# Sinkhorn attention and max-out layer on one core: W2 turned by DMA instead of TensorE, its loads gated, and the first item in another order

## The chip, the core and the metric

The kernel runs on one NeuronCore of a Trainium2 chip. The metric is the time on the device in microseconds, the median of several executions. A NeuronCore has five engines with instruction streams of their own, joined by semaphores: TensorE (PE; PEld is its weight load), VectorE (DVE), ScalarE (ACT), GpSimd (POOL) and SyncE (SP). Sixteen DMA engines move data between HBM, the main memory, and SBUF, the memory on the core; GpSimd and SyncE issue almost all of the DMAs here. Matmuls write to PSUM, from where DVE or ACT copies results to SBUF.

## The reference

```python
P = sort_net                                   # (4, 8, 8, 8)
for _ in range(5):
    P = exp(P - max(P, -1))
    P = P / (sum(P, -1) + 1e-9)
    P = P / (sum(P, -2) + 1e-9)
k_sorted = einsum('bhij,bhjcd->bhicd', P, k_b) # k, v: (4, 8, 768, 64) in 8 blocks of 96
v_sorted = einsum('bhij,bhjcd->bhicd', P, v_b)
attn = softmax(q_b @ k_sorted^T / 8)           # within each block of 96
x = (attn @ v_sorted) -> (3072, 512)           # heads side by side
out = maximum(x @ w1, x @ w2) @ w_out          # w1, w2: 512 x 1024, w_out: 1024 x 512
```

All inputs and the output are float32; the kernel's matmul operands are bfloat16, cast during the loads.

## The kernel before, in words

The batch has four items (b = 0 to 3); each gives 768 tokens. The work of one item is this chain:

- `sort_k(b, t)`, t = 0 to 2: 32 small matmuls that multiply k by a block-diagonal matrix made from P (L458), and a copy to kT (DVE or ACT). The t-th sort needs only the t-th third of the loaded k.
- `turn_v` reorders v within each partition (L245 on ACT, L250 on DVE), and `sort_v`, `sort_v_pair` or `sort_v_halved` sort it (L479, L523, L500). A sort of v takes single columns out of all 96 rows of a block, so it needs every turn.
- `q_transposes`: on TensorE for items 0 and 1 (L433), by DMA for items 2 and 3 (L419).
- `scores(b, u)`, u = 0 to 7 (L548), the exponential on ACT (L556), `values(b, u)` (L575), and the division on DVE (L586, L592), which gives x. The first four u belong to the first half of the tokens, the last four to the second.
- `x_transposes(b, t)`: on TensorE for item 0 (L613), by DMA on SP's queue for the others (L605). Two u make one t. The products of the first token half need t = 0 and 1, those of the second t = 2 and 3.
- `moe_h(b, ch, t)` (L677), then `moe_out(b, ti, part)` (L704).

The layer uses max(h1, h2) = relu(x(W1 - W2)) + x W2. So W2 is subtracted from W1 in SBUF (`w_difference`, L231, by quarters of 256 columns: two on GpSimd, two on DVE), relu is taken of the products, and W2 W_out is made once as the matrix wc (`w_product(dmt)`, L657) and applied to x next to W_out. For `w_product`, W2 must be transposed (w2T). In the kernel before, `w2_transposes(t, eng)` does that: 16 matmuls of 128 columns against the identity (L638) and one copy of 2048 columns by `evac`, for each half of W2's 1024 columns (steps tw0 and tw1).

Everything stands in program order by hand; each engine takes its instructions in that order. `evac` gives a copy to ACT or DVE by a running load count unless an engine is named. PSUM has four tiles for everything (`ps`).

The stages, with what sets their order:

- The start: five sinkhorn rounds on DVE and ACT (`sinkhorn(it)`, L264 to L283), with ACT turning v of item 0 between them. TensorE multiplies zeros meanwhile (`keep_streaming`, L82): 86 matmuls of 126 columns, then six of 512 columns in each of the last two rounds. GpSimd issues, in this order, v, k and q of item 0, then after two mask copies (L763) the first two quarters of W2 and W1, the selections, the other halves of both, W_out, two differences, and k of item 1 (L767 to L777).
- The front: item 0, by the list `front` (L783 to L789): k, v sorts, tq q transposes, SC scores, VA values, tx x transposes, tw W2 transposes, h products with a letter a or b for the two halves of their accumulation, diff the differences on DVE, pe the block-diagonal matrices of the other items, and F zeros of 512 columns put ahead of the next step that takes them. A trailing A or D names the engine of the copy. Before the last 26 steps, q of item 1, v of items 1 and 2 and k of item 2 are issued (L830 to L834); behind the front, q of item 2 into W2's buffer (L838).
- The rest: for each item, a list of units (L909 to L933). For item 0 there are eight empty ones, four of `w_product` (n = 8 to 11) and twelve of `moe_out` (n = 12 to 23); for the later items eight of `moe_h` and twelve of `moe_out`. Behind unit n the steps of a tail are put: `first_tail` holds item 1's attention and the sorting of v of items 1 and 2 (`sort_v_pair`), `second_tail` item 2's attention and v of item 3. KS is the three key sorts, TQ the q transposes, TURN the turns, VS the sorts of v, SC, VA and TR scores, values and x transposes.

All loads are issued by GpSimd, and so go through one queue of DMAs; outputs and transposing DMAs go through SP's.

Of the kernel before, what the change touches and what calls it, by code (L numbers as in the profile page):

```python
# [11 lines left out]
BF16 = mybir.dt.bfloat16  # L12
# [4 lines left out]
def kernel(  # L17
# [16 lines left out]
    nc = tc.nc  # L34
# [34 lines left out]
    def ps_bf16(name):  # L69
        return psum.tile([128, 2048], BF16, tag="ps", name=name)  # L70
# [48 lines left out]
    kT = {}  # L119
# [511 lines left out]
    w2T = big.tile([128, NFB, DMODEL], BF16, tag="w2T", name="w2T")  # L631
    wc = big.tile([128, HP, DMODEL], BF16, tag="wc", name="wc")

    def w2_transposes(t, eng):
        ps = ps_bf16("tw_ps")
        for n in range(16):
            fb, dmt = t * 4 + n // 4, n % 4
            nc.tensor.matmul(  # L638
                ps[:, n * 128 : (n + 1) * 128],
                w2_sb[:, dmt, fb * 128 : (fb + 1) * 128],  # L640
                ident,
                is_transpose=True,
                start=True,
                stop=True,
            )
        return lambda: evac(
            w2T[:, t * 4 : t * 4 + 4, :].rearrange("p f d -> p (f d)"),
            ps,
            2048,
            two_x=True,  # L650
            eng=eng,
        )

    def w_product(dmt):
# [95 lines left out]
        return SC, VA, TR  # L750

    first, second, both = slice(0, 64), slice(64, 128), slice(0, 128)
    keep_streaming(ps_f32("fill_ps"), 86 * 126, most=126)
    for it in range(5):
        sinkhorn(it)
        if it < 3:
# [5 lines left out]
    for c, n, m in [(2, 2, 0), (4, 3, 1)]:  # L762
# [1 line left out]
            out=maskJ[:, c : c + n],  # L764
            in_=maskJ[:, m].to_broadcast([128, NB, n]).transpose([0, 2, 1]),
        )
    for t in range(2):  # L767
        load_w_columns(w2_sb, moe_w2, t, t + 1)
        load_w_columns(w1_sb, moe_w1, t, t + 1)
    for b in range(1, B):  # L770
        selections(b)
    load_w_columns(w2_sb, moe_w2, 2, 4)
    load_w_columns(w1_sb, moe_w1, 2, 4)
    load_w(wo_sb, moe_w_out)
    w_difference(0, nc.gpsimd)
    w_difference(1, nc.gpsimd)
    load_k(1)  # L777
    turn_v(first, "A", 36, 56)
    turn_v(first, "A", 56, 80)
    block_diagonals_first()  # L780
    turn_v(first, "D", 80, 96)

    front = """  # L783
        k0D k1A k2D v1D v2A v3A tq0D v0A tq1D SC1 SC0 F1
        SC2 VA1 SC5 VA0 SC3 F2 VA2 SC4 F0 tx0D SC6 VA3
        SC7 h00a VA4 tx1A tw0D h01a VA5 h01bA diff2 h00bA VA7 tx2A
        tw1A h02a VA6 h02bA h11a diff3 tx3A h12a h03a h12bD h10a h10bA
        pe2 h11bD h03bA h13a h13bA
    """.split()  # L789
    fills = [0]  # L790

    def fills_due():
# [3 lines left out]
    def front_step(step):  # L796

        eng = step[-1] if step[-1] in "AD" else None
        name = step[:-1] if eng else step
        kind = name.rstrip("0123456789ab")  # L800
        n = [int(x) for x in name if x.isdigit()]
        if kind == "F":
            fills[0] = 512
        elif kind == "k":
            sort_k(0, n[0], 640 if step == front[0] else 0, eng)
        elif kind == "v":
            sort_v(0, n[0], 0, eng)
        elif kind == "tq":
            q_transposes(0, n[0], eng)
        elif kind == "SC":  # L810
            scores(0, n[0], fills_due())
        elif kind == "VA":
            values(0, n[0], fills_due())
        elif kind == "tx":
            x_transposes(0, n[0], eng)
        elif kind == "tw":
            w2_transposes(n[0], eng)()
        elif kind == "diff":
            w_difference(n[0])
        elif kind == "pe":  # L820
            block_diagonals([(0, 2), (0, 3), (1, 1), (1, 2), (1, 3)], 2)
        elif name[-1] == "a":
            moe_h_products(0, n[0], n[1], (0, 2), fills_due())
        else:
            moe_h(0, n[0], n[1], eng, (1, 3))

    for step in front[:-26]:
        front_step(step)

    load_q(1)  # L830
    for piece in range(2):
        for b in (1, 2):
            load_v(b, which=piece)
    load_k(2)  # L834

    for step in front[-26:]:
        front_step(step)
# [7 lines left out]
    def sorts_and_scores(b):  # L845
# [6 lines left out]
    TURN = [lambda c=c: turn(both, c) for c in (0, 24, 48, 72)]  # L852
    first_tail = {
        7: KS,
        9: [TQ[0], TURN[0]],
        10: [SC[0], TQ[1], TURN[1]],
        11: SC[1:4] + TURN[2:4] + [lambda half=half: load_v(3, half=half) for half in range(2)],
        12: VS[0:3],
        13: VS[3:6],
        14: VS[6:8] + [SC[4]],  # L860
        15: [VA[0], lambda: pair_q(2, 0)],
        16: [VA[1], lambda: pair_q(2, 1)],
        17: SC[5:8] + [TR[0]],
        18: [VA[2]],
        19: [VA[3], TR[1]],
        20: [VA[4]],
        21: [VA[5], TR[2]],
        22: [VA[6], VA[7], TR[3]],
    }
    SC, VA, TR, KS = sorts_and_scores(2)  # L870
    VS = [lambda t=t: sort_v_halved(3, t) for t in range(4)]
    TURN = [lambda c=c: turn(both, c) for c in (0, 24, 48, 72)]
    second_tail = {
        0: [lambda: q_transposes(2, 0), lambda: q_transposes(2, 1)],
        2: KS,
        4: SC[0:2],
        5: [VA[0]],
        6: SC[2:4] + [TURN[0]],
        7: [VA[1], TR[0]],
        8: [VA[2], TURN[1]],  # L880
        9: [VA[3], TR[1], TURN[2]],
        10: SC[4:7],
        11: [VA[4], TURN[3]],
        12: [VA[5], TR[2], lambda: load_k(3), lambda: load_q(3)],
        13: [VA[6]],
        14: SC[7:8] + VS[0:2],
        15: [VA[7], TR[3]],
        16: VS[2:4],
        17: [lambda: pair_q(3, 0)],
        18: [lambda: pair_q(3, 1)],  # L890
    }
    SC, VA, TR, KS = sorts_and_scores(3)
# [69 lines left out]
```

The softmax here doesn't subtract the row's maximum and nothing guards it: scores larger than these inputs give would overflow.

## Time and profile before

| | |
|---|---|
| median of 8 runs | 166.58 us (166.16 to 169.9) |
| the profiled execution's own time | 166.71 us |
| its span | 164.9 us |
| granted TensorE clock | 0.997 |
| instructions | 4563 |
| data moved by DMA | 23.90 MB, 145 GB/s over the span |
| loads, through GpSimd's queue | 11040 packets, 13.37 MB, 48.3% of 16 engines |
| outputs and transposing DMAs, through SP's queue | 19200 packets, 10.17 MB, 26.3% |

The span goes from the first to the last instruction of one profiled execution; the execution's own time is 1.8 us more. Times inside are microseconds from the span's start. The page cuts the span in 40 slices of 4.1 us; a digit is the busy share of a slice in tenths. The chain of work that ended last is followed back from the last instruction, at each step to what released it. "From issue to landing" is the time from the start of a DMA's issuing instruction until its data are there.

### The profile page before, as it was taken

What the parts mean: (1) busy time and instruction counts of PE and PEld (TensorE: products, weight loads), DVE (VectorE), ACT (ScalarE), POOL (GpSimd) and SP (SyncE); (2) the same over time, 40 slices, a digit from 0 to 9 for tenths busy, and PEclk for the clock granted to TensorE, in tenths of its full rate; (3) what the DMA queues carried; (4) which work ended last, traced back from release to release, by engine and by line L of the source; (5) the groups of instructions that cost most, each with busy time, mean ns of one, the idle gap of its engine ahead of it and who ended that gap; (6) DMA issues with size and microseconds to landing.
All of it is one profiled execution on the core that took longest, in us unless ns stands there. A gap on an engine that the chain in (4) does not pass through costs nothing.

```text
span 164.9 us, 4563 instructions
## 1 busy us (share of the span) xinstructions
PE 159.4 (97%) x2018; PEld 96.5 (59%) x2018; DVE 76.2 (46%) x169; ACT 83.1 (50%) x102; POOL 32.7 (20%) x59
## 2 busy tenths in 40 slices
PE   7999799999999999999999999999999999999992
PEld 7958578756555555557655554575655546654451
DVE  4869778546375574535277763250642420000011
ACT  3585894927239847055752353457447206642020
POOL 7989587140205000000014010000000000000000
PEclk9999999999999999999999999999999999999998
DMA  3999999999999995688425999990025294000333
GB/s 41 202 207 197 198 208 204 210 204 220 211 205 209 218 234 105 175 116 205 102 19 105 187 182 225 195 228 16 0 52 175 50 164 142 0 0 0 127 131 127
DMA packets 30405, 23.90 MB, mean 145 GB/s; under 512 B 16753, under 2 KB 25201, under 8 KB 30385
## 3 DMA queue, kind: packets, MB, share of 16 engines
q0 software_dynamic: 11040, 13.37, 48.3%
q1 hardware_dynamic: 19200, 10.17, 26.3%
q8 instruction: 16, 0.26, 0.6%
q10 hardware_dynamic: 144, 0.07, 0.1%
q14 instruction: 5, 0.03, 0.1%
HBM read 26.75 MB, written 6.29 MB: 200 GB/s over the span
## 4 chain that ended last, share of the span: by engine, by line
PE 95%; ACT 1%; issue 1%; DVE 1%
PE out_ps L704 38%; PE h_ps L677 26%; PE fill_ps L82 6%; PE o_ps L575 5%; PE wc_ps L657 4%; PE k_ps L458 4%; PE s_ps L548 4%; PE tq_ps L433 2%; PE v_ps L479 1%; PE v_ps L523 1%; PE tw_ps L638 1%; ACT e L556 1%; PE tx_ps L613 1%; PE v_ps L500 1%; DVE qT L110 1%
## 5 line engine op out<-in xcount | busy, mean ns | idle before, releaser
L704 PE MATMUL out_ps<-wo_sb,g 128*128 128x512 bf16 (+2 forms) x200 | 48.3, 371 | 0.1
L677 PE MATMUL h_ps<-xT,w_sb 128*128 128x384 bf16 x256 | 44.5, 326 | 0.0
L677 PEld LDWEIGHTS <-w_sb 128*128 128x128 bf16 x256 | 24.0, 98 | 15.6
L556 ACT ACTIVATE e<-s_ps 96x768 bf16<-96x768 f32 x32 | 23.9, 804 | 14.0 <-PE s_ps L548 13.8
L691 ACT ACTIVATE g<-h_ps 128x768 bf16<-128x768 f32 x27 | 21.8, 811 | 17.4 <-PE h_ps L677 17.3
L704 PEld LDWEIGHTS <-g 128*128 128x128 bf16 x200 | 17.1, 97 | 15.8
L704 PE MATMUL out_ps<-wc,xT 128*128 128x512 bf16 (+2 forms) x100 | 24.8, 370 | 0.0
L108 ACT COPY o<-out_ps 128x1024 f32<-128x1024 f32 x10 | 10.1, 1012 | 28.0 <-PE out_ps L704 25.2
L592 DVE TENSOR_TENSOR x<-o_ps,rs 96x512 bf16<-96x512 f32 x32 | 22.0, 687 | 1.1
L704 PEld LDWEIGHTS <-xT 128*128 128x128 bf16 x100 | 9.6, 97 | 11.2
L575 PEld LDWEIGHTS <-e 96*128 96x128 bf16 x256 | 11.8, 97 | 5.9 <-DVE v_sb L110 0.2
L586 DVE RECIPROCAL rs<-o_ps 96x8 f32<-96x8 f32 x32 | 6.4, 200 | 18.1 <-PE o_ps L575 17.9
L739 DVE COPY o<-out_ps 128x512 f32<-128x512 f32 (+1 forms) x2 | 1.2, 625 | 27.6 <-PE out_ps L704 27.6
L575 PE MATMUL o_ps<-v_sb,e 96*128 96x65 bf16 x256 | 12.9, 193 | 0.0
L110 DVE CAST kT<-k_ps 128x1024 bf16<-128x1024 f32 x7 | 8.3, 1216 | 9.3 <-PE k_ps L458 9.3
L108 ACT CAST v_sb<-v_ps 96x1024 bf16<-96x1024 f32 x10 | 9.8, 1013 | 2.4 <-PE v_ps L479 0.9
L693 DVE TENSOR_SCALAR g<-h_ps 128x768 bf16<-128x768 f32 x5 | 4.8, 956 | 10.8 <-PE h_ps L677 10.8
L110 DVE CAST v_sb<-v_ps 96x1024 bf16<-96x1024 f32 x6 | 7.3, 1218 | 5.1 <-PE v_ps L523 2.2
L548 PE MATMUL s_ps<-qT,kT 64*128 64x96 bf16 x256 | 8.6, 204 | 1.1 <-PE o_ps L575 0.8
L548 PEld LDWEIGHTS <-kT 64*128 64x128 bf16 x256 | 6.1, 94 | 5.9 <-issue 3.6
L160 POOL DMA_DIRECT2D v_raw<-in_k_dram x3 | 2.5, 833 | 35.2 <-DVE v_dc L250 31.4
L82 PE MATMUL fill_ps<-fill 128*128 128x126 bf16 x86 | 7.7, 278 | 1.2 <-DVE fill L73 1.2
(95 smaller groups left out, 143.3 us busy)
## 6 DMA issues: line engine op xcount, KB each, us to landing
out_dram<-o SPq DMA_DIRECT2D x11, 512.0 KB, 3.1
v_raw<-in_v_dram POOLq DMA_DIRECT2D x8, 384.0 KB, 12.5
k_raw<-in_k_dram POOLq DMA_DIRECT2D x9, 256.0 KB, 10.0
w_sb<-in_moe_w_dram POOLq DMA_DIRECT2D x4, 256.0 KB, 9.5
w_sb<-in_moe_w_dram POOLq DMA_DIRECT2D x2, 512.0 KB, 11.0
wo_sb<-in_moe_w_out_dram POOLq DMA_DIRECT2D x2, 512.0 KB, 14.5
v_raw<-in_v_dram POOLq DMA_DIRECT2D x3, 256.0 KB, 4.9
q_raw<-in_q_dram POOLq DMA_DIRECT2D x4, 192.0 KB, 9.1
```

Of the source, the lines that this page charges most:

```text
L82: nc.tensor.matmul(ps[:, 0:w], w0, fill[:, 0:w], start=True, stop=True)
L108: nc.scalar.copy(out=out_ap, in_=in_ap)
L110: nc.vector.tensor_copy(out=out_ap, in_=in_ap)
L458: nc.tensor.matmul(ps[r0 : r0 + 64, m * 64 : (m + 1) * 64], kv[r0 : r0 + 64, t * 16 + m, :], bd_k[b][r0 : r0 + 64, :], start=True, stop=True,)
L548: nc.tensor.matmul(ps[:, h2 * 512 + ii * 128 : h2 * 512 + ii * 128 + BLK], kT[b][rows, (hp * 8 + i) * BLK : (hp * 8 + i) * BLK + 128], rhs ...
L556: nc.scalar.activation(out=e[:, 0 : 8 * BLK].rearrange("p (t c r) -> p t c r", t=8, r=R), in_=ps[0:BLK] .rearrange("p (t f) -> p t f", t=8 ...
L575: nc.tensor.matmul(ps[:, h2 * 512 + ii * 65 : h2 * 512 + (ii + 1) * 65], e[:, (h2 * 4 + ii) * BLK : (h2 * 4 + ii) * BLK + 128], v_sb[:, m0 ...
L592: nc.vector.tensor_tensor(out=x, in0=ov[:, :, :, 0:D], in1=rs.to_broadcast([BLK, 2, 4, D]), op=ALU.mult,)
L657: nc.tensor.matmul(ps[:, 0:512], w2T[:, fb, dmt * 128 : (dmt + 1) * 128], wo_sb[:, fb, :], start=(fb == 0), stop=(fb == NFB - 1),)
L677: nc.tensor.matmul(h_ps[ch, t][:, m * 512 : m * 512 + TCH], w1_sb[:, hp, fb * 128 : (fb + 1) * 128], xT[:, b % 2, ch, hp % 2, hp // 2, :], ...
L691: nc.scalar.activation(out=g, in_=src, func=AF.Relu)
L704: nc.tensor.matmul(dst, g_tiles[b, ch, m // 2][:, m % 2, off : off + 128] if m < NFB else xT[:, b % 2, ch, hp % 2, hp // 2, off : off + 12 ...
```

## The change

- `w2_transposes(dmt)` becomes one DMA transpose on SP's queue: 128 rows (of the 512) of W2 by 1024 columns, for each of the four dmt, written to w2T. The steps tw0 and tw1, their 32 matmuls and their two copies go.
- GpSimd's loads are gated by three small copies to a new tile `seen`. The first reads the last sinkhorn result; behind it come the first quarter of W2 and the selections of items 1 and 2. The second reads the first sorted keys; behind it come the other loads of W1 and W2 (now the second half of W1 ahead of that of W2), the selection of item 3, W_out, the four transposes (on SP), the differences and k of item 1. The third reads the w2T columns that the second transpose writes; behind it come q of item 1 (now in four DMAs), v of items 1 and 2 (now in four pieces each) and q of item 2.
- k of item 2 is loaded later, behind unit 16 of item 0's units.
- The front list has another order, beginning with the second token half, and four F instead of three; F now adds up.
- The zeros at the start: 92 matmuls of 118 columns.
- The tails of items 0 and 1 are placed anew: of item 1's attention nearly everything stands later in the list of units.

```diff
--- before.py
+++ after.py
@@ -631,24 +631,10 @@
     w2T = big.tile([128, NFB, DMODEL], BF16, tag="w2T", name="w2T")
     wc = big.tile([128, HP, DMODEL], BF16, tag="wc", name="wc")
 
-    def w2_transposes(t, eng):
-        ps = ps_bf16("tw_ps")
-        for n in range(16):
-            fb, dmt = t * 4 + n // 4, n % 4
-            nc.tensor.matmul(
-                ps[:, n * 128 : (n + 1) * 128],
-                w2_sb[:, dmt, fb * 128 : (fb + 1) * 128],
-                ident,
-                is_transpose=True,
-                start=True,
-                stop=True,
-            )
-        return lambda: evac(
-            w2T[:, t * 4 : t * 4 + 4, :].rearrange("p f d -> p (f d)"),
-            ps,
-            2048,
-            two_x=True,
-            eng=eng,
+    def w2_transposes(dmt):
+        nc.sync.dma_start_transpose(
+            out=w2T[:, :, dmt * 128 : (dmt + 1) * 128],
+            in_=w2_sb[:, dmt, :],
         )
 
     def w_product(dmt):
@@ -750,7 +736,7 @@
         return SC, VA, TR
 
     first, second, both = slice(0, 64), slice(64, 128), slice(0, 128)
-    keep_streaming(ps_f32("fill_ps"), 86 * 126, most=126)
+    keep_streaming(ps_f32("fill_ps"), 92 * 118, most=118)
     for it in range(5):
         sinkhorn(it)
         if it < 3:
@@ -764,29 +750,24 @@
             out=maskJ[:, c : c + n],
             in_=maskJ[:, m].to_broadcast([128, NB, n]).transpose([0, 2, 1]),
         )
-    for t in range(2):
-        load_w_columns(w2_sb, moe_w2, t, t + 1)
-        load_w_columns(w1_sb, moe_w1, t, t + 1)
-    for b in range(1, B):
-        selections(b)
-    load_w_columns(w2_sb, moe_w2, 2, 4)
-    load_w_columns(w1_sb, moe_w1, 2, 4)
-    load_w(wo_sb, moe_w_out)
-    w_difference(0, nc.gpsimd)
-    w_difference(1, nc.gpsimd)
-    load_k(1)
     turn_v(first, "A", 36, 56)
     turn_v(first, "A", 56, 80)
     block_diagonals_first()
+    seen = const.tile([128, 3, 2], BF16, tag="seen", name="seen")
+    nc.gpsimd.tensor_copy(out=seen[0:G, 0], in_=p_bf[:, NB - 1, NB - 2 :])
+    load_w_columns(w2_sb, moe_w2, 0, 1)
+    selections(1)
+    selections(2)
     turn_v(first, "D", 80, 96)
 
     front = """
-        k0D k1A k2D v1D v2A v3A tq0D v0A tq1D SC1 SC0 F1
-        SC2 VA1 SC5 VA0 SC3 F2 VA2 SC4 F0 tx0D SC6 VA3
-        SC7 h00a VA4 tx1A tw0D h01a VA5 h01bA diff2 h00bA VA7 tx2A
-        tw1A h02a VA6 h02bA h11a diff3 tx3A h12a h03a h12bD h10a h10bA
-        pe2 h11bD h03bA h13a h13bA
+        k1A k0A v1D k2A v2A v0D tq0D v3A tq1D SC4 SC5 F2
+        F3 VA4 SC6 SC7 VA5 F0 SC0 VA6 SC1 VA7 F1 SC3
+        tx2D SC2 tx3D VA1 h10a VA0 VA2 h10bA h11a tx0A h11bA diff3
+        VA3 diff2 h13a h01a tx1D h03a h13bD h03bD h01bA h12a pe2 h00a
+        h02a h00bD h02bA h12bA
     """.split()
+
     fills = [0]
 
     def fills_due():
@@ -800,7 +781,7 @@
         kind = name.rstrip("0123456789ab")
         n = [int(x) for x in name if x.isdigit()]
         if kind == "F":
-            fills[0] = 512
+            fills[0] += 512
         elif kind == "k":
             sort_k(0, n[0], 640 if step == front[0] else 0, eng)
         elif kind == "v":
@@ -813,8 +794,6 @@
             values(0, n[0], fills_due())
         elif kind == "tx":
             x_transposes(0, n[0], eng)
-        elif kind == "tw":
-            w2_transposes(n[0], eng)()
         elif kind == "diff":
             w_difference(n[0])
         elif kind == "pe":
@@ -824,14 +803,29 @@
         else:
             moe_h(0, n[0], n[1], eng, (1, 3))
 
-    for step in front[:-26]:
+    front_step(front[0])
+    c0 = int(front[0][1]) * 16
+    nc.gpsimd.tensor_copy(out=seen[:, 1], in_=kT[0][:, c0 : c0 + 2])
+    load_w_columns(w1_sb, moe_w1, 0, 1)
+    load_w_columns(w2_sb, moe_w2, 1, 2)
+    selections(3)
+    load_w_columns(w1_sb, moe_w1, 1, 2)
+    load_w_columns(w1_sb, moe_w1, 2, 4)
+    load_w_columns(w2_sb, moe_w2, 2, 4)
+    load_w(wo_sb, moe_w_out)
+    for dmt in range(HP):
+        w2_transposes(dmt)
+    w_difference(0, nc.gpsimd)
+    w_difference(1, nc.gpsimd)
+    load_k(1)
+    nc.gpsimd.tensor_copy(out=seen[:, 2], in_=w2T[:, NFB - 1, 254:256])
+    for step in front[1:-26]:
         front_step(step)
 
-    load_q(1)
-    for piece in range(2):
+    load_q(1, True)
+    for piece in range(4):
         for b in (1, 2):
-            load_v(b, which=piece)
-    load_k(2)
+            load_v(b, 4, which=piece)
 
     for step in front[-26:]:
         front_step(step)
@@ -852,41 +846,39 @@
     TURN = [lambda c=c: turn(both, c) for c in (0, 24, 48, 72)]
     first_tail = {
         7: KS,
-        9: [TQ[0], TURN[0]],
-        10: [SC[0], TQ[1], TURN[1]],
-        11: SC[1:4] + TURN[2:4] + [lambda half=half: load_v(3, half=half) for half in range(2)],
-        12: VS[0:3],
-        13: VS[3:6],
-        14: VS[6:8] + [SC[4]],
-        15: [VA[0], lambda: pair_q(2, 0)],
-        16: [VA[1], lambda: pair_q(2, 1)],
-        17: SC[5:8] + [TR[0]],
-        18: [VA[2]],
-        19: [VA[3], TR[1]],
-        20: [VA[4]],
-        21: [VA[5], TR[2]],
-        22: [VA[6], VA[7], TR[3]],
+        12: [TQ[0]],
+        13: [SC[0], TQ[1]],
+        14: SC[1:4] + TURN[0:2],
+        15: SC[4:5] + TURN[2:4] + [lambda half=half: load_v(3, half=half) for half in range(2)],
+        16: VS[0:3] + [lambda: load_k(2)],
+        17: VS[3:6],
+        18: VS[6:8],
+        19: [VA[0]],
+        20: [VA[1]] + SC[5:8],
+        21: [VA[2], VA[3], TR[0], TR[1]],
+        22: [VA[4], VA[5], TR[2]],
+        23: [VA[6], VA[7], TR[3]],
     }
     SC, VA, TR, KS = sorts_and_scores(2)
     VS = [lambda t=t: sort_v_halved(3, t) for t in range(4)]
     TURN = [lambda c=c: turn(both, c) for c in (0, 24, 48, 72)]
     second_tail = {
-        0: [lambda: q_transposes(2, 0), lambda: q_transposes(2, 1)],
+        0: [lambda: pair_q(2, 0), lambda: pair_q(2, 1)],
+        1: [lambda: q_transposes(2, 0), lambda: q_transposes(2, 1)],
         2: KS,
-        4: SC[0:2],
-        5: [VA[0]],
-        6: SC[2:4] + [TURN[0]],
-        7: [VA[1], TR[0]],
-        8: [VA[2], TURN[1]],
-        9: [VA[3], TR[1], TURN[2]],
+        5: SC[0:2],
+        6: [VA[0], TURN[0]],
+        7: SC[2:4],
+        8: [VA[1], TR[0], TURN[1]],
+        9: [VA[2], TURN[2]],
         10: SC[4:7],
-        11: [VA[4], TURN[3]],
-        12: [VA[5], TR[2], lambda: load_k(3), lambda: load_q(3)],
-        13: [VA[6]],
+        11: [VA[3], TR[1], TURN[3]],
+        12: [VA[4], lambda: load_k(3), lambda: load_q(3)],
+        13: [VA[5], TR[2]],
         14: SC[7:8] + VS[0:2],
-        15: [VA[7], TR[3]],
+        15: [VA[6]],
         16: VS[2:4],
-        17: [lambda: pair_q(3, 0)],
+        17: [VA[7], TR[3], lambda: pair_q(3, 0)],
         18: [lambda: pair_q(3, 1)],
     }
     SC, VA, TR, KS = sorts_and_scores(3)
```

## The prediction

> **What bounds the kernel now.** I read the engine table first, then the chain of work that ended last, then the windows and the DMA view of the first 75 us. The table says TensorE:
>
> ```profile
> PE 159.4 (97%) x2018; PEld 96.5 (59%) x2018; DVE 76.2 (46%) x169; ACT 83.1 (50%) x102; POOL 32.7 (20%) x59
> ...
> DMA  3999999999999995688425999990025294000333
> ```
>
> TensorE is idle for 164.9 - 159.4 = 5.5 us. Of that, 1.2 us lie before its first matmul and about 3 us behind the last one. What any edit of order can still win inside is little; work taken off TensorE counts in full, as long as nothing else becomes late. The DMA row is the second fact: the 16 DMA engines are full from slice 2 to slice 15, that is to 62 us. The chain shows the stretch that the change rewrites:
>
> ```profile
> 25.22 0.90 PE tw_ps L638 x16
> ...
> 28.93 0.90 PE tw_ps L638 x16
> ...
> 38.57 1.64 PE k_ps L458 x96
> 40.20 3.56 PE wc_ps L657 x16
> ...
> 69.49 0.49 PE o_ps L575 x16
> 69.98 1.30 PE out_ps L704 x6
> 71.27 3.90 PE h_ps L677 x24
> ```
>
> The two groups of W2 transposes are on the chain, with matmuls on both sides. Item 1's keys are sorted at 38.57, W2·W_out starts at 40.20, and item 1's first product with W1 starts at 71.27. These three times are my milestones. The loads beside them:
>
> ```profile
> 24.23 1.66 POOL L160 DMA_DIRECT2D k_raw<-in_k_dram  x3
> 25.86 0.92 POOL L143 DMA_DIRECT2D q_raw<-in_q_dram  x1
> DMA to landing us min/median/max: 10.0/10.3/10.7
> ```
>
> The last line is for the second and third key load of item 1, issued at 24.8 and 25.3: the third lands at 25.3 + 10.7 = 36.0, and is needed at about 39.6, as the third of the three sorts. In the same way q of item 1 lands at 40.7 and the last of v at 47.8 (issued 32.8, 15.0 us).
>
> What transposing DMAs do beside loads is seen later in the same trace, from the DMA view of two windows of 2 us: 108:110, transposes alone, and 92:94, one transpose beside a key load:
>
> ```profile
> q1 hardware_dynamic: 1699, 0.43, 114.6%
> ```
> ```profile
> q0 software_dynamic: 167, 0.32, 95.5%
> q1 hardware_dynamic: 187, 0.04, 20.1%
> ```
>
> Columns are packets, MB and share of 16 engines. Alone, transposes move 850 packets of 256 bytes per us. Beside the load they get 94 per us (24 GB/s), about one packet for each load packet of 2 KB, while the load keeps 0.32 MB in 2 us = 160 GB/s of the 205 to 217 it has alone.
>
> [...]
>
> **The change, part by part.**
>
> Removed: 32 transposes on TensorE, 2 x 0.90 = 1.80 us on the chain, and their copies, 1.23 us on DVE and 1.87 us on ACT, both hidden behind products with W1. Nothing takes their place: TensorE is busy in the whole of 21:38.
>
> Zero matmuls: 92 x 118 = 10,856 columns against 86 x 126 = 10,836. They end near 8.7 us, ahead of the late zeros and the sinkhorn result at 11.2: 0. The four fills of the front are 512 columns each (0.22 us), one more than before: +0.22 on TensorE, or nothing where it waits anyway. I take 0.1.
>
> Front order: the same sorts, scores, values, x transposes and products. The 0.29 + 0.35 + 0.50 us of idle at 18 to 21 come from eight exponentials (0.80 each) and x products (0.69 + 0.20 each) that must come before enough products with W1 exist; this is so in either order, item halves being swapped. I take 0, with -0.5 to +0.7 as bounds. Sum: the front ends 1.80 - 0.1 = 1.7 us earlier, at 36.9.
>
> W loads: GpSimd now waits for the last sinkhorn result (11.2) before W2's first quarter, and for the first sorted keys (about 14.0: matmuls until 12.7, an ACT copy of 1.01) before the others. Queued behind these waits are the selections of items 1 to 3, the W loads, two differences (2.12 each) and item 1's keys. The DMA engines have 2.36 MB of v, k and q of item 0 ahead, which at 205 GB/s last until about 15.5; with W2's quarter until 16.7. The next quarter is issued by 14.8. So no gap, and W1's first two quarters land near 19.5 and 22.0 as before (differences started at 19.50 and 22.17). The eight loads take 0.74 each; the last is issued at about 20.0, so the differences run 20.0 to 24.3 and item 1's keys are issued at 24.3, as before. Cost 0; if GpSimd came 2 us late, DMA would stand still for that long and every later landing move by it.
>
> W2's DMA transposes: four of 256 KB, 4096 packets in all, on SP's queue, which has nothing else until the first output at about 54. They wait for all of W2, which now lands last of the two, at 27.2. At 28.4 loads still have 0.39 MB of W_out and 0.79 MB of keys: 1.18 MB at 160 GB/s last until 35.8, so the third key load lands at 35.8 + 1.8 = 37.6, needed at 36.9 + 1.1 = 38.0. Just in time: 0, where the loads' loss is at most that of the row; 1.3 if they fell to 130 GB/s. By 35.8 some 700 transposing packets are through; the rest run alone, the first of the four done at 36.2, the second at 37.4, the last at 39.9. With 1.5 us of landing they serve products that start at 38.5, 40.2, 41.9 and 43.7.
>
> Loads behind them: GpSimd waits for the second transpose, about 38.9, then issues q of item 1 (four, 0.75 each), v of items 1 and 2 (eight, 0.53 each) and q of item 2. Data from about 40.6; q is in by 44.4 + 1.8 (first needed at 46.7), v by 51.8 + 1.8 = 53.6. The last turn on DVE, 0.82, ends at 54.5; the sorts of values now start behind the fifth output part, near 55.1. So 6 us later than before, and the later places in the order cover it.
>
> Boundary to item 1: here the change has a price. In before, the fourth value product ends at 65.1, its x transpose is issued at 66.37 and lands at 69.9, and it is needed at 71.6. After, only two output parts (1.30 each) and four value products (0.24 each) and two matmuls (0.16 each) follow: 3.9 us. The way there is 0.9 + 0.9 us of DVE (two x back to back, partly begun) = 1.6, and 2.8 to 3.5 from issue to landing: 4.4 to 5.1. TensorE waits 0.5 to 1.2 us; I take 0.8.
>
> Sum, likeliest: -1.7 + 0.8 = -0.9 us. The profiled execution took 166.71 (span 164.9), the median is 166.58: **165.7**.
>
> **The rivals.**
>
> (1) Slower: the boundary transposes behind the loads. q, v, q, v and k of items 1 to 3 that must come after 40.6 are 5.5 MB; at 217 GB/s (4.72 MB landed between 40.7 and 62.4 in before) that is 25.4 us, with a second output write 1.5, and v of item 3 waiting for the turns 1.1: the loads end at about 68.6, two us more if rates fall. A transpose issued beside them trickles at 94 packets per us; in before one took 8.4 us beside q of item 3. Then x lands only when the loads are through: 68.6 + 0.9 + 1.8 = 71.3, up to 74. Against the 69.9 at which TensorE wants it that is 1.4 to 4. It decides from 1.7 us, a landing past 71.6: with 3 us, 166.6 - 1.7 + 3.0 = 167.9. For it: the DMA row is full to 62 already, and 1.05 MB (5 us) is added. Against it: large rows of v move at up to 220 GB/s.
>
> (2) Cancelled: the waits just equal the saving, by 1.7 us at the boundary, or by the key load (1.3) and a short boundary wait: 166.5, no measurable change.
>
> (3) The boundary is free, the loads being done by 66 and DVE ahead, and the new order closes 0.3 of the idle at 18 to 21: 166.6 - 2.0 = 164.6.
>
> **How the numbers follow.** Likeliest case 0.45, at 165.7, by itself 165.1 to 166.2; rival (1) 0.26, at 167.9 (166.9 to 169.5); rival (2) 0.15; rival (3) 0.14. A change within 0.3% (0.5 us) is about what a measurement of this kernel can't tell from none. Faster: 0.14 and nearly all of 0.45, together 0.57; same 0.17; slower 0.26. The range leaves out half of rival (3) and a third of (1): 164.6 to 168.2.
>
> **What would show it.** Right: no W2 transpose on TensorE; item 1's key sort on the chain near 36.9 without idle ahead of its third part; the third key load landing before 38.0; the second W2 transpose landing near 39; item 1's first product at about 70.4 with a wait of 0.8. Wrong: idle at the key sort (loads share more evenly than the row shows); idle before W2·W_out (transposes starved); value sorts waiting for turns; an x transpose of item 1 that takes over 6 us. The prediction fails most easily in the loads' end near 68.6.

## The result and the profile after

The changed kernel takes 172.32 us (median of 11 runs, 170.68 to 174.17), the kernel before 166.5 us (median of 32 runs, 166.12 to 169.9). The ratio is 1.0332, 95% interval 1.0311 to 1.0353: slower by 3.3%, and outside the predicted range. (Ratios here leave disturbed runs out, medians don't; so a ratio can differ from the quotient of two medians.)

The profiled execution of after took 170.68 us (span 168.9, granted clock 0.999). All others ran at a mean granted clock of 0.98 to 0.99 and took 171.35 us or more. So there are two amounts to explain: 4.0 us that the profiled execution shows against 166.71, and another 1.6 us by which the median lies above it.

The engine table and the DMA row of after:

```profile
PE 158.1 (94%) x1993; PEld 93.5 (55%) x1993; DVE 75.3 (45%) x169; ACT 81.0 (48%) x100; POOL 38.0 (22%) x69
...
DMA  3999999999999999999605999984025253000333
```

TensorE does 1.3 us less than before, but is idle for 168.9 - 158.1 = 10.8 us instead of 5.5. The DMA engines are full to the end of slice 19 (80 us) instead of 62 us.

The timeline of TensorE in after, from which I keep the milestones and the longer waits (columns: start, duration, line and operation, count, idle before it and what ended it):

```profile
28.93 1.47 PE L663 MATMUL h_ps<-xT,w_sb 128*128 128x384 bf16 x8 [1.00 <-DVE w_sb L231]
...
37.54 1.71 PE L458 MATMUL k_ps<-bd,k_raw 64*64 64x64 bf16 x96
39.17 7.08 PE L643 MATMUL wc_ps<-wo_sb,w2T 128*128 128x512 bf16 x32
...
56.30 0.87 PE L523 MATMUL v_ps<-bd,v_dc 64*128 64x64 bf16 x48 [0.39 <-DVE v_dc L250]
...
65.72 0.34 PE L548 MATMUL s_ps<-qT,kT 64*128 64x96 bf16 x8 [0.57 <-DVE x L592]
...
74.44 4.34 PE L663 MATMUL h_ps<-xT,w_sb 128*128 128x384 bf16 x24 [2.92 <-DMA xT<-x]
```

W2·W_out follows the key sort with no wait. Then come three waits that the kernel before doesn't have, the longest at the first product of item 1. In the same view of before, the key sort starts at 38.50, and the first product at 71.11 without a wait:

| us from the start | before | predicted | after |
|---|---|---|---|
| key sort of item 1 | 38.50 | 36.9 | 37.54 |
| its third load lands | 36.0 | 37.6 | 37.8 |
| second W2 transpose lands | | 38.9 | 39.2 |
| last of v of items 1 and 2 lands | 47.8 | 53.6 | 55.4 |
| loads' end | 62.4 | 68.6 | 73.0 |
| first product of item 1 | 71.11 | 70.4 | 74.44 |

The chain of waits of after passes through DMAs where before it ran on TensorE:

```profile
29.57 9.65 DMA w2T<-w_sb
...
39.51 2.80 POOL q_raw L143 x4
42.31 13.07 DMA v_raw<-in_v_dram x2
...
69.53 5.47 DMA xT<-x
...
75.05 3.73 PE h_ps L663 x22
```

W2's transpose holds back GpSimd, GpSimd the v loads, those the sorts of v, and the second x transpose ends the stretch. The DMA view of 64:70, just ahead (packets, MB, share of 16 engines), then the output issued at 63.83 and the transpose issued at 65.69, with the us from issue to landing:

```profile
q0 software_dynamic: 389, 0.99, 84.7%
q1 hardware_dynamic: 195, 0.40, 19.4%
out_dram<-o SPq DMA_DIRECT2D x1, 512.0 KB, 9.9
```
```profile
xT<-x SPq DMA_TRANSPOSE x1, 8.6
```

The transpose issued at 65.69 needs 8.6 us, the next one, at 69.53, the 5.47 us of the chain, where before one needed 3.5. It does not trickle beside the loads: 0.40 MB in 195 packets are 2 KB a packet, the rows of an output, and a transpose has packets of 256 bytes (0.25 MB in 1020 packets in 74:75). SP's queue moves the 512 KB of output first, about one row for one load packet (133 against 136 in 68:70), and its first packet of 256 bytes comes at 71.0. In before, where no load runs at that time, the output issued at 65.94 lands in 3.0. The order is the same in the profiles of after_again, pe_w2 and new_tails below: item 1's first x transpose is issued at 65.0, 67.3 and 67.6, and the first small packet comes at 70.4, 72.3 and 72.6. The loads that are still running, v of item 3 and k of item 2, are issued late, by GpSimd's timeline (in brackets, what it waited for):

```profile
39.28 0.18 POOL L821 COPY seen<-w2T 128x2 bf16<-128x2 bf16 x1 [13.11 <-DMA w2T<-w_sb]
...
53.58 0.88 POOL L169 DMA_DIRECT2D v_raw<-in_v_dram  x1 [3.48 <-DVE v_dc L250]
56.53 1.55 POOL L169 DMA_DIRECT2D v_raw<-in_v_dram  x3 [2.07 <-DVE v_dc L250]
58.05 1.67 POOL L160 DMA_DIRECT2D k_raw<-in_k_dram  x3
```

The account of the profiled execution: the key sort comes 0.96 us earlier. From there to the first product it is 36.90 us instead of 32.61, so 4.29 more: 2.92 + 0.57 + 0.39 = 3.88 are the waits shown, 0.4 is spread. After it another 0.7. Together -0.96 + 4.29 + 0.7 = +4.0.

### The profile page after: what moved, and what is told of

It is laid out like the page before. It is cut to its first block, busy times and chain, and to the rows that moved or that the text cites. A ratio compares the mean times of both kernels' runs of the same rounds, so it can differ in the third digit from the quotient of the medians.

```text
span 168.9 us, 4529 instructions
## 1 busy us (share of the span) xinstructions
PE 158.1 (94%) x1993; PEld 93.5 (55%) x1993; DVE 75.3 (45%) x169; ACT 81.0 (48%) x100; POOL 38.0 (22%) x69
## 2 busy tenths in 40 slices
DMA packets 34995, 24.93 MB, mean 148 GB/s; under 512 B 21088, under 2 KB 29536, under 8 KB 34976
## 4 chain that ended last, share of the span: by engine, by line
PE 62%; DMA 24%; DVE 5%; POOL 4%; ACT 1%; issue 1%; SPq 1%
PE out_ps L690 33%; PE h_ps L663 19%; DMA v_raw<-in_v_dram 8%; DMA w_sb<-in_moe_w_dram 6%; DMA w2T<-w_sb 6%; DMA xT<-x 3%; PE o_ps L575 3%; PE k_ps L458 2%; PE s_ps L548 2%; POOL w_sb L189 2%; POOL q_raw L143 2%; PE v_ps L523 1%; DMA p_sb<-in_sort_net_dram 1%; SPq L635 1%; DVE colsum L276 1%
## 5 line engine op out<-in xcount | busy, mean ns | idle before, releaser
L575 PEld LDWEIGHTS <-e 96*128 96x128 bf16 x256 | 11.1, 97 | 6.1 <-ACT e L556 0.9
L575 PE MATMUL o_ps<-v_sb,e 96*128 96x65 bf16 x256 | 12.4, 193 | 0.2 <-ACT e L556 0.2
L110 DVE CAST v_sb<-v_ps 96x1024 bf16<-96x1024 f32 x7 | 8.5, 1221 | 5.7 <-PE v_ps L523 2.8
L110 DVE CAST kT<-k_ps 128x1024 bf16<-128x1024 f32 x5 | 5.9, 1221 | 9.6 <-PE k_ps L458 9.6
L169 POOL DMA_DIRECT2D v_raw<-in_v_dram x15 | 8.3, 581 | 8.1 <-DVE v_dc L250 5.5
L108 ACT CAST v_sb<-v_ps 96x1024 bf16<-96x1024 f32 x9 | 8.9, 1008 | 2.4 <-PE v_ps L523 0.9
```

Of the source, the lines that this page charges most:

```text
L108: nc.scalar.copy(out=out_ap, in_=in_ap)
L110: nc.vector.tensor_copy(out=out_ap, in_=in_ap)
L169: nc.gpsimd.dma_start(out=v_raw[r0 : r0 + 64, m * n : (m + 1) * n], in_=v_src[b, :, m * n : (m + 1) * n],)
L575: nc.tensor.matmul(ps[:, h2 * 512 + ii * 65 : h2 * 512 + (ii + 1) * 65], e[:, (h2 * 4 + ii) * BLK : (h2 * 4 + ii) * BLK + 128], v_sb[:, m0 ...
```

## Experiments

My first theory: the boundary wait is the loss, and it comes from the 1.05 MB that W2's transposes move and from the third gate, which push the loads of items 1 to 3 to the boundary, where the x transposes land late beside them. Rival: the new places of the steps make it by themselves. Second question: what lifts the median above the profile.

**The same kernel again, for the clock.** No edit.

> The changed kernel as it is, as the control of this group. Theory (the loss is a wait of TensorE ahead of item 1's first products with W1, for x transposes that trickle beside late loads, and TensorE's granted clock falls behind that wait[...]): about 172.3 us; in a profile with a mean granted clock of 0.99 the clock is low in the few us right behind the wait and nowhere else. Rival (the clock falls somewhere else, or everywhere by 1%): the low stretch is not at the boundary.

172.78 us, ratio 1.0374 (1.0338 to 1.0411). This time the profile caught an execution with the lower clock. Its timeline of TensorE, and then the window 75:79 (us, busy time and count of PE, PEld, DVE, ACT, POOL; granted clock, DMA share, GB/s):

```profile
74.03 6.05 PE L663 MATMUL h_ps<-xT,w_sb 128*128 128x384 bf16 x24 [3.16 <-DMA xT<-x]
```
```profile
75.00:79.00 4.00, 4.00 (x16) 1.96 (x15) 0.00 (x0) 0.93 (x2) 0.00 (x0) 0.57 1.06 238
```

The same 24 products take 6.05 us instead of 4.34: the mean clock of these 4 us is 0.57 (0.60 in 75:76, 0.50 in 76:78, 0.69 in 78:79, so half from about 75.2 to 78.6), where the first profile has 1.00 in the same window. That is 1.7 us, about the distance of the median. So this execution loses twice here: 3.16 us of idle time, and 1.7 us by the lowered clock behind it.

**W2 back on TensorE, the rest of the change kept.** Without W2's DMAs and the third gate.

```diff
-    for dmt in range(HP):
-        w2_transposes(dmt)
...
-    nc.gpsimd.tensor_copy(out=seen[:, 2], in_=w2T[:, NFB - 1, 254:256])
...
-        tx2D SC2 tx3D VA1 h10a VA0 VA2 h10bA h11a tx0A h11bA diff3
-        VA3 diff2 h13a h01a tx1D h03a h13bD h03bD h01bA h12a pe2 h00a
+        tx2D SC2 tx3D VA1 h10a VA0 VA2 h10bA h11a tx0A tw0D h11bA diff3
+        VA3 diff2 h13a h01a tx1D tw1A h03a h13bD h03bD h01bA h12a pe2 h00a
```

> The changed kernel with W2 turned on TensorE again (tw0 and tw1 in the front, as in the kernel before) and without the third gate; order of the front, gates of the W loads and later places of item 1's steps kept. Theory: the loads run on as before and end near 62, so the boundary wait shrinks to what DVE and the landing need (0.5 to 1.2 us) and the clock holds: 166.5 to 168. Rival (the new places alone, with only two output parts between the last values and item 1, make the wait): 171 or more.

173.16 us, 1.0385 (1.033 to 1.0439). My theory fell: without any W2 DMA the kernel is just as slow, and the wait is still there, followed by a clock as low as in after_again (0.57 in 76:80, 0.50 in 77:79):

```profile
75.12 6.00 PE L677 MATMUL h_ps<-xT,w_sb 128*128 128x384 bf16 x24 [1.97 <-DMA xT<-x]
```

**Only the third gate taken out.**

```diff
-    nc.gpsimd.tensor_copy(out=seen[:, 2], in_=w2T[:, NFB - 1, 254:256])
```

> The changed kernel without the third gate: q of item 1 and v of items 1 and 2 are issued right behind item 1's keys, beside the four DMA transposes of W2. Theory (a transpose gets about one packet of 256 bytes for each load packet): the transposes trickle at 94 packets per us or fewer, the first lands near 40, the fourth long after; the products W2 W_out wait: over 180. Rival (the gate is what costs, and the DMA engines would share evenly): the loads come 8 us earlier, the boundary wait goes: 167 to 168.

186.86 us, 1.1185 (1.1106 to 1.1265), as expected. The timeline of TensorE:

```profile
40.03 1.90 PE L643 MATMUL wc_ps<-wo_sb,w2T 128*128 128x512 bf16 x8 [1.21 <-DMA w2T<-w_sb]
53.20 7.60 PE L643 MATMUL wc_ps<-wo_sb,w2T 128*128 128x512 bf16 x24 [11.27 <-DMA w2T<-w_sb]
```

Beside q and v W2's four transposes land 9.6 to 24.0 us after their issue; in after, where the gate holds these loads back, it is 4.3 to 10.2 us, and W2·W_out has no wait. The gate is what makes W2's DMAs bearable; what it delays is their price.

**Item 1's first two x transposes on TensorE.** No x transpose is then left in the crowd at the boundary.

```diff
-        if b:
+        if b > 1 or (b == 1 and t > 1):
```

> The changed kernel with item 1's first two x transposes on TensorE instead of DMA: 16 matmuls of 96 columns more (0.7 us) and two copies. Theory: the boundary wait for them goes and the clock holds: 172.3 - 3.3 - 1.7 + 0.7 = about 168. Rival (something else, such as DVE or item 2's keys, is as late there): 171 or more.

170.52 us, 1.0277 (1.0193 to 1.0361). The first product starts at 73.23 instead of 74.44, with the clock at 0.998. That is less than expected, since a wait for DVE takes the place of the DMA's:

```profile
69.31 0.51 PE L613 MATMUL tx_ps<-ident,x 96*128 96x96 bf16 x8 [1.27 <-DVE x L592]
```

From the key sort (36.60 in this profile) to the first product it is 4.0 us more than before: waits of 0.93 for the turns of v, 0.57 and 1.27 for x, and 0.7 of added matmuls make up most of it. Item 1's attention ends so close to its use that even with no DMA between them the first product comes 2.1 us later than before. So I put the parts on the kernel before one by one. **Only the new tails** (the diff of `first_tail` and `second_tail` in the change, with k of item 2 behind unit 16), all else as before:

```diff
-    load_k(2)
...
-        9: [TQ[0], TURN[0]],
-        10: [SC[0], TQ[1], TURN[1]],
-        11: SC[1:4] + TURN[2:4] + [lambda half=half: load_v(3, half=half) for half in range(2)],
...
+        14: SC[1:4] + TURN[0:2],
+        15: SC[4:5] + TURN[2:4] + [lambda half=half: load_v(3, half=half) for half in range(2)],
+        16: VS[0:3] + [lambda: load_k(2)],
```

> The kernel before with nothing but the new places of the steps of items 1 and 2 (tails, with k of item 2 loaded behind unit 16). Theory now (after the run with W2 back on TensorE was no faster: the new places alone turn v late on DVE, so that the loads of v of item 3, which wait for these turns, and of k of item 2 behind them run into the boundary, and the x transposes of item 1, placed closer to their use, land late): 170 to 173, with a wait ahead of item 1's first product. Rival (the places are harmless where the loads are early, and it was the front order or the gates that cost): 166 to 167.5.

172.71 us, 1.0284 (1.0178 to 1.0389): the tails alone lose about as much as the whole change. (TensorE is slower in this profile's front too, ahead of anything that the tails move: eight matmuls of scores take 0.50 us at 21.14 and 22.55, and 0.34 at 20.51 and 24.93; the mean clock is 0.98. But the one execution at a mean clock of 1.0 took 170.5, about as long as the 170.68 of after.) GpSimd's timeline, one window of all engines, and the boundary on TensorE:

```profile
55.93 0.56 POOL L169 DMA_DIRECT2D v_raw<-in_v_dram  x1 [20.70 <-DVE v_dc L250]
```
```profile
52.00:56.00 4.00, 3.84 (x67) 2.36 (x68) 2.79 (x4) 1.92 (x3) 0.07 (x1) 1.00 0.00 0
```
```profile
75.70 5.72 PE L677 MATMUL h_ps<-xT,w_sb 128*128 128x384 bf16 x24 [2.25 <-DMA xT<-x]
```

v of item 3 goes into the buffer that the turns of v of items 1 and 2 read. With the turns four to five units later, GpSimd waits 20.7 us, and k of item 2 is queued behind. The DMA engines stand still (0 GB/s in 52:56; before moves 220 there), and the loads then run at 242 GB/s in 64:72, just where item 1's x is transposed.

**The whole change with the old tails**: the change's diff of both tails taken back.

```diff
+    load_k(2)
...
-        12: [TQ[0]],
-        13: [SC[0], TQ[1]],
-        14: SC[1:4] + TURN[0:2],
...
+        9: [TQ[0], TURN[0]],
+        10: [SC[0], TQ[1], TURN[1]],
+        11: SC[1:4] + TURN[2:4] + [lambda half=half: load_v(3, half=half) for half in range(2)],
+        12: VS[0:3],
```

> The changed kernel with the old places of items 1 and 2 (k of item 2 loaded behind v). W2 by DMA and the third gate stay, so q and v of item 1 land 5 and 7 us later than before. Theory: TensorE then waits ahead of item 1's q transposes and sorts of v instead of at the boundary, some 5 us, and the sum is no better: 171 to 174. Rival (the tails are the whole loss, whatever the loads do): 165 to 167.

174.32 us, 1.0432 (1.0352 to 1.0513), just above the 171 to 174 that I expected. With the late loads of the W2 DMAs the old places come too early. The two largest waits on TensorE:

```profile
42.72 0.53 PE L433 MATMUL tq_ps<-ident,q_raw 128*64 128x128 bf16 x12 [0.90 <-DMA q_raw<-in_q_dram]
...
55.87 1.46 PE L523 MATMUL v_ps<-bd,v_dc 64*128 64x64 bf16 x48 [3.96 <-DVE v_dc L250]
```

So the two parts belong together: W2's DMAs need the late places, and the late places lose at the boundary what was to be won.

**Front order and the first two gates alone** (the edits of W2 on TensorE and of the old tails, both from above, on after; v and q stay in finer pieces).

> W2 on TensorE, no third gate, the old places of items 1 and 2, k of item 2 loaded where it was; so of the change there remain the front order, the first two gates and the finer loads. Theory (the tails are the cost): 166.5 to 167.7, the front ending some 0.7 us later than before because a difference waits for the half of W2 that lands last. Rival (front order or gates cost more): over 169.

167.74 us (16 runs), 1.0052 (1.0032 to 1.0072): just above the expected range, a small loss. The key sort comes at 39.51, 1.0 later than before, and 1.02 us is a wait for the DVE difference, as in after.

**W2 by DMA alone in the kernel before, without gates**; tw0 and tw1 are out of the list.

```diff
     load_w(wo_sb, moe_w_out)
+    for dmt in range(HP):
+        w2_transposes(dmt)
     w_difference(0, nc.gpsimd)
```

> The kernel before with W2 turned by four DMA transposes, issued behind the W loads, and nothing else: no gates, old order, old places. Theory (a transpose gets a packet for a packet beside loads that go on to 62 us): the products W2 W_out wait as they did without the third gate: 180 to 190. Rival (DMA has room for 1 MB more): 165 to 166.

189.29 us, 1.136 (1.1275 to 1.1445), as expected: TensorE waits 10.32 and 6.99 us for w2T.

The next four split the tails, the front and the W2 transfer further. **New tails with k of item 2 where it was:**

```diff
+    load_k(2)
...
-        16: VS[0:3] + [lambda: load_k(2)],
+        16: VS[0:3],
```

> The kernel before with the new tails, but k of item 2 loaded where it was (behind v of items 1 and 2), so that it uses the 8 us in which DMA stood still with the new tails. Theory (x transposes of item 1 trickle until the loads behind the turns are through): those loads are 0.8 MB less, end near 68 instead of 72, and the boundary wait shrinks by 1 to 3 us, the clock holding in part: 168 to 171. Rival (the wait is DVE's, with six divisions in three units): no change, 172 to 173.

168.28 us, 1.0097 (1.0066 to 1.0128). Of the tails' loss, 3 us by the ratios (1.0284 - 1.0097) or 4.4 by the medians belong to this one load: 768 KB that filled the boundary. With the execution of new_tails at a mean clock of 1.0 it is 170.5 against 168.28, some 2.2 us; the others of new_tails had 0.97 to 0.99.

**And the turns and v of item 3 early too:**

```diff
+        9: [TURN[0]],
+        10: [TURN[1]],
+        11: TURN[2:4] + [lambda half=half: load_v(3, half=half) for half in range(2)],
...
-        14: SC[1:4] + TURN[0:2],
-        15: SC[4:5] + TURN[2:4] + [lambda half=half: load_v(3, half=half) for half in range(2)],
+        14: SC[1:4],
+        15: SC[4:5],
```

> As the kernel with the new tails and early k of item 2, and the turns of v and the loads of v of item 3 back at their old units 9 to 11; only q transposes, scores, sorts of v, values and x transposes of item 1 keep the new places. Theory (late loads make the loss, closeness to the boundary only adds what DVE and a landing without contention need): 166.7 to 167.8, wait 0.3 to 1.2 us, clock held. Rival (six divisions and the near use are the loss): 170 or more.

168.14 us, 1.0088 (1.0054 to 1.0123): the clock held, but the time lies above the expected range. v of item 3 and k of item 2 are now as early as before, yet 1.7 us stay lost against 166.45. The boundary on TensorE:

```profile
72.56 3.74 PE L677 MATMUL h_ps<-xT,w_sb 128*128 128x384 bf16 x22 [0.52 <-DMA xT<-x]
```

The second transpose lands in 2.8 us here, with 117 GB/s moved in 64:72 (242 in new_tails), and TensorE still waits 0.52 for it. A wait of 0.57 for x at the last scores comes on top, as in after. Together 1.09 of the 1.4 us by which the span is longer (166.3 against 164.9): the price of closeness alone.

**Only the new front order on the kernel before.** W2's transposes stay on TensorE, behind tx0 and tx1.

```diff
+        k1A k0A v1D k2A v2A v0D tq0D v3A tq1D SC4 SC5 F2
+        F3 VA4 SC6 SC7 VA5 F0 SC0 VA6 SC1 VA7 F1 SC3
+        tx2D SC2 tx3D VA1 h10a VA0 VA2 h10bA h11a tx0A tw0D h11bA diff3
+        VA3 diff2 h13a h01a tx1D tw1A h03a h13bD h03bD h01bA h12a pe2 h00a
+        h02a h00bD h02bA h12bA
```

> The kernel before with nothing but the new order of the front (the W2 transposes put beside the first two x transposes of the second group, four fills that add up). W loads ungated and in their old order. Theory (the order is neutral, what the run with old tails lost came from W2's last half landing at 28.1 behind the gates instead of 27.2): 166.3 to 167.0. Rival (the order itself asks for the last difference too early): 167.5 to 167.8, a wait for the difference of 0.5 to 1 us.

168.46 us, 1.0113 (1.008 to 1.0147). My theory fell here too: I had taken the order to cost nothing. TensorE, and then DVE:

```profile
30.66 1.47 PE L677 MATMUL h_ps<-xT,w_sb 128*128 128x384 bf16 x8 [1.02 <-DVE w_sb L231]
```
```profile
28.78 1.23 DVE L110 COPY w2T<-tw_ps 128x2048 bf16<-128x2048 bf16 x1 [0.93 <-PE tw_ps L638]
29.92 0.68 DVE L231 TENSOR_TENSOR w_sb<-w_sb 128x1024 bf16<-128x1024 bf16 x1
```

The key sort comes at 40.15, 1.65 later than before; 1.02 of that is this wait. The difference of W1's last quarter is needed earlier in this order, and here it stands behind a copy of w2T on DVE. In after that copy is gone, and the same wait of 1.00 comes from the load of W2 instead, as its DVE timeline says:

```profile
28.18 0.69 DVE L231 TENSOR_TENSOR w_sb<-w_sb 128x1024 bf16<-128x1024 bf16 x1 [1.08 <-DMA w_sb<-in_moe_w_dram]
```

**One of the four W2 transposes by DMA, on the kernel before**; TensorE does 24 of the 32 matmuls.

```diff
-        for n in range(16):
-            fb, dmt = t * 4 + n // 4, n % 4
+        for n in range(12):
+            fb, dmt = t * 4 + n // 3, n % 3
...
+    nc.sync.dma_start_transpose(out=w2T[:, :, 384:512], in_=w2_sb[:, 3, :])
```

> The kernel before with only the last quarter of W2's transposes (the 128 rows of dmt 3, needed by the last product at 47.4) done by one DMA, issued behind the W loads; the other three quarters stay on TensorE, 24 matmuls instead of 32. Theory (a transpose beside loads gets about 94 packets per us: 1024 packets from about 26 are through by 38 to 40, well ahead of 47; loads lose 1.3 us, for which 1.7 to 3 us are free): 0.45 us less on TensorE, 166.0 to 166.4. Rival (even one transpose makes a load late): 167 or more.

167.86 us, 1.0082 (1.0039 to 1.0124). My theory fell, the rival holds: even 256 KB beside full DMA engines costs more than the 0.45 us of TensorE that it saves. The waits on TensorE:

```profile
39.21 0.69 PE L458 MATMUL k_ps<-bd,k_raw 64*64 64x64 bf16 x32 [0.24 <-DMA k_raw<-in_k_dram]
...
44.13 0.86 PE L433 MATMUL tq_ps<-ident,q_raw 128*64 128x128 bf16 x24 [0.68 <-DMA q_raw<-in_q_dram]
...
52.68 0.88 PE L523 MATMUL v_ps<-bd,v_dc 64*128 64x64 bf16 x48 [0.82 <-DVE v_dc L250]
```

They sum to 1.74; 1.74 - 0.45 = 1.29, and the median is 1.4 above before. (The span of this profile is 1.0 longer.)

The last three ask whether the full change can be saved by keeping loads away from the boundary. **k of item 2 early in it** (same edit as above, on after):

> The full change with k of item 2 loaded right behind v of items 1 and 2. Theory (the DMA engines are full to 72 us there, so that the order within the loads moves little: v of item 3 takes the place of k): 170.5 to 172.5, boundary wait of 2 to 3 us. Rival (k of item 2 alone is the trouble, as in the kernel with only the new tails, where moving it back won 4.4 us): 168 to 169.

172.45 us, 1.0287 (1.0182 to 1.0392): nothing moves, as expected. v of item 3 now lands where k did, and TensorE waits 2.71 us. With 1.05 MB more to move, this exchange of two loads wins nothing, which points to their sum.

**v of item 3 behind the second x transpose of item 1**, by a small copy on GpSimd that reads xT, as the other gates do; its issue moves from unit 15 to unit 21.

```diff
+    def v3_behind_x():
+        last = const.tile([128, 2], BF16, tag="last", name="last")
+        nc.gpsimd.tensor_copy(out=last, in_=xT[:, 1, 0, 1, 1, TCH - 2 :])
...
-        21: [VA[2], VA[3], TR[0], TR[1]],
+        21: [VA[2], VA[3], TR[0], TR[1], v3_behind_x]
+        + [lambda half=half: load_v(3, half=half) for half in range(2)],
```

> The full change with k of item 2 early and v of item 3 issued only when the second x transpose of item 1 has landed (a small GpSimd copy that reads it). Theory (loads that still run at the boundary make the wait): the transposes land 2.8 to 3.5 us after issue, the boundary wait is about 1 us, the clock holds; v of item 3 lands near 80, just ahead of its turns: 166.5 to 168.5. Rival (W2's transposes and the third gate make the loss by themselves): 171 or more.

178.18 us, 1.0641 (1.054 to 1.0743), some 10 us above what I expected. The boundary obeys: the first two transposes land in 3.4 us or less, the first product starts at 72.01, and the wait for the second transpose is 0.48. But the load only moves on to the next transposes; item 1's fourth, issued at 73.90, lands 13.3 us later. TensorE, and the DMA view of 76:82:

```profile
87.25 4.64 PE L663 MATMUL h_ps<-xT,w_sb 128*128 128x384 bf16 x14 [7.17 <-DMA xT<-x]
```
```profile
q0 software_dynamic: 184, 0.93, 93.1%
q1 hardware_dynamic: 173, 0.04, 5.0%
```

About packet for packet, but against load packets of 5 KB in the mean: 173 / 6 = 29 transposing packets per us.

**The same with h13 three steps later in the front**, so that its difference is there in time.

```diff
-        VA3 diff2 h13a h01a tx1D h03a h13bD h03bD h01bA h12a pe2 h00a
+        VA3 diff2 h01a tx1D h03a h13a h13bD h03bD h01bA h12a pe2 h00a
```

> As the one before, and in the front the products h13 that need the last difference stand behind h01, tx1 and h03. Theory: the wait of 0.2 to 1.0 us for the last half of W2 goes: 0.3 to 1.0 us less than the one before, 165.8 to 168. Rival (another wait takes its place): the same as the one before.

177.96 us, 1.0653 (1.0579 to 1.0727). The wait for the difference (1.61 in the profile of v3_gated) is gone, one of 0.73 for x takes its place, and the key sort starts at 37.39 instead of 38.02. The time is the same as without this edit, as the rival said. The first product comes at 71.06, against 71.11 in before. So even with the boundary nearly free (0.49 us of waiting), nothing of the change's gain is left by then.

No version that I ran beats the kernel before.

## Why the prediction was wrong

**The step that failed is the boundary, "I take 0.8"**, and behind it the assumption that "the later places in the order cover it". They did cover the sorts of v, which wait only 0.39 us. But the same places release v of item 3 and k of item 2 later, these loads still run at the boundary, and there TensorE waited 2.92 us in the first profile and 3.16 in the second, where a lowered clock took 1.7 more. Rival (1), with a chance of 0.26, named the loads at the boundary; its 167.9 was too small as well.

*Removed work*: right. 32 transposes are off TensorE, and W2·W_out starts without a wait on data that land at 39.2 (38.9 predicted).

*Key sort at 36.9*: half right. It came at 37.54, so 0.96 us were won and not 1.7. "Cost 0" for the W loads was too low: the second half of W2 lands at 28.1 instead of 27.2. The new order asks for its difference sooner than before, which I had not followed up, and TensorE waits 1.00. This wait differs between executions: in profiles with the same front and the same loads up to there it is 0.20 (tr_pe, old_tails, key sort at 36.6) to 1.61 (v3_gated, 38.02). Against that the idle time at 18 to 21 fell from 0.28 + 0.85 to 0.20 + 0.22 us, which I had put into rival (3). The gated loads move 176 GB/s in 16:21 where before moves 198; I had argued that there is no gap.

*Third key load*: right, 37.8 against 37.6, and no wait. The gates hold the order that the step assumed. Its 1.8 us of landing are what before shows: at 205 GB/s, the 1.18 MB from 28.4 on are through at 34.2, and the third load landed at 36.0. The 1.5 us for W2's transposes were only my estimate; item 1's first x transpose in before moved its last bytes at 64.15 and landed at 64.7.

*Loads' end at 68.6*: too early by 4.4 us; this is where the prediction said it would fail most easily. The loads were 5.50 MB, as computed. But SP's queue moved 1.31 MB in the same stretch (the end of W2's transposes, output and x), and with 0.06 MB of other traffic all ran at 6.87 MB / 32.4 us = 212 GB/s. At that rate 1.31 MB are 6.2 us; I had allowed 2.6 for outputs and turns together. The 217 GB/s was a misreading as well: in 40.7:62.4 of before the loads' queue moved 4.20 MB, not 4.72, which is 193 GB/s; only with SP's 0.42 MB and the rest is it 216. So it is about the rate of all traffic, and the forecast used it for the loads alone.

*Boundary*: the working for closeness was sound, 0.5 to 1.2 us: with nearly quiet DMA engines (early_turns) 0.52 is waited there. The landing of 2.8 to 3.5 us in it was taken from a place without loads. By my own numbers the first transpose, issued at 65.69, fell before the loads' end, so that price could not hold: 8.6 us, and a wait of 2.92. I had put this into a rival and kept the quiet price in the forecast. The rival's way was not quite right either. It has the transpose trickle at 94 packets per us; in after no transposing packet of item 1 moves before 71.0, and the output issued ahead of it on SP's queue is still moving then, 133 packets beside 136 of the loads in 68:70.

*What no case held*: the lowered clock after the wait, 1.7 us in after_again; all executions of after but the profiled one have a mean clock of 0.99 or less, which agrees. The forecast's sum with the measured terms is 166.6 - 1.0 (front) + 4.3 (key sort to first product) + 0.7 (behind it) + 1.6 (clock) = 172.2.

*Cover that wasn't*: I took the new tails as cover for late loads. Alone they cost 2.8% (new_tails): more than half of it from one load that they push to the boundary and the lowered clock (0.97 to 0.99 in three of four executions), some 1.5 us from the places that are left in early_turns (0.88%). W2's DMAs without them cost as much (old_tails). The losses don't add up, since each alone fills the same boundary or opens the same waits.

**Left open.** How the small loss of pe_w2_old_tails divides between gates and order: front_order alone took more (168.46), so the gates may cost nothing. What lowers the clock. Whether item 1's x transposes would land in time with the output issued behind them, and not ahead of them in SP's queue, was not tried. A version with v of item 3 behind item 2's q transposes, with later turns, was not tried.

## What to carry to other kernels

Before moving work from the bounding engine to DMA, look at the DMA row in the stretch that follows. If it is full, expect what came here: with 1.05 MB of transposes, their gate and the later steps the loads' end went from 62.4 to 73.0, a transpose beside a load moved 94 packets per us where it moved 850 alone, and item 1's first x transpose, issued behind an output of 512 KB, took 8.6 us to land. A step moved later also moves the loads that wait for its buffer, and those land on whatever is tight there: follow each moved consumer to the load that it releases. A price of a transfer holds only for the company in which it was measured: item 1's x transposes landed in 2.8 to 4.5 us in before and in 3.8 to 8.6 in after.

## What the hardware showed beyond expectation

- The granted clock was 0.50 behind two of the waits at the boundary: in 76:78 behind 3.16 us (after_again) and in 77:79 behind 1.97 us (pe_w2). It was 1.00 in 75:79 behind the 2.92 us in the profile of after. And it was 0.50 in 22:28 in the profile of new_tails_k2_early, behind waits of 0.29 and 1.06 us. So the length of a wait did not tell here what the clock would do, and what does is not shown.
- How many packets a DMA transpose got beside a load differed from load to load: 94 per us in 92:94 of before, beside load packets of 2 KB (187 against 167), and 29 per us in 76:82 of v3_gated, beside load packets of 5 KB in the mean (173 against 184). Alone it was 850 per us (1699 packets in 108:110 of before). In the two windows with a load both queues moved about as many packets; why, the traces do not show.
